# One-hot rows in groups, an earlier trial gather, early weights spread over more turns, and one copy on another engine

## The chip, the cores and the metric

The kernel runs on one core of one Trainium2 chip. The metric is device time in microseconds (us) of one execution. The engines are PE (TensorE), DVE (VectorE), ACT (ScalarE), POOL (GpSimd) and SP (SyncE, which here only issues DMAs); each takes its instructions in order, and they meet through semaphores. A queue letter behind an engine's name in the rows (ACTq, POOLq) is its sequencer, which waits, branches or issues.

## What is computed

Block-causal attention over 8 batches of 8 heads, 576 tokens and 64 columns a head, then a mixture of 8 experts over the 4608 tokens. Each expert takes at most `capacity` = 80 of the tokens that the gate sends to it, those with the largest gate weight; all other rows of the output are zero.

```python
scores = q @ k.T / 8, masked by blocks of 64          # per batch and head
attn   = softmax(scores) @ v
x      = attn.transpose(0, 2, 1, 3).reshape(4608, 512)
logits = x @ w_gate;  expert = argmax(logits);  g = softmax(logits)[expert]
for e in range(8):
    tok = the (at most) 80 tokens of expert e with the largest g
    out[tok] = g[tok] * (relu(x[tok] @ w1[e]) @ w2[e])
```

## The kernel before

**Attention.** The 64 heads are worked as 32 pairs, four pairs a batch. A loop runs over turns `i`; turn `i` holds steps of several pairs, written out in the list `TURN` as (distance, step): scores and softmax of pair i, transposes and values of pair i-1, preparation of q and k (`prep`) for pair i+2, loads of v for pair i+2 (`load_v`, three POOL DMAs), of k for pair i+5 (`load_k`, four POOL DMAs) and of q for pair i+6 (SP). The order on every engine is that of the program text (`tc.manual_schedule`). In every fourth turn and the one behind it POOL also stores the finished x of a batch to `xs` in HBM (`store_x`, L389, two and two DMAs). SP stores a batch's 1/sums (`rs`, L395 and L396), and clears the output from turn 4 on, 512 KB at a time, in three turns of four.

`prep` transposes q on DVE (L626) and scales it on POOL (L629, tile `T`); PE's scores (L648) read it. POOL's `pad` (L602, tile `VZ`) copies parts of v for the values (L784). The five transposes at L743 come once in a turn.

**Early weights.** Four of the sixteen weight matrices (2 MB each) are loaded by POOL during attention: `EARLY` says how many quarters are issued at the head of which turn (n = 32 is the number of pairs). At the head of a turn stands `early(EARLY.get(i, 0))`; a call with 1 to 3 issues single quarters of 512 KB at L346, one with 4 a whole matrix as one DMA. All later weights are issued by SP (L325).

**The last pair.** In turn n, ahead of the copy of the last pair's `xT` out of PSUM (`take` of "values", L792 on ACT or L794 on DVE, by the table `TAKE`), stand `recip` (DVE, L379 and L380) and `store(nc.scalar)`, which issues the two `rs` stores of the last batch from ACT's queue (L395, L396). Behind the copy come DVE's `flip` (L384), POOL's last four `xs` stores (L389), and the last logits (PE L406), which ACT copies to `lgT` (L412).

**Selection.** From the gate weights each of the 128 partitions keeps its 12 largest candidates. The rank of a candidate is counted among the others: by DVE for the first five (L977, `cnt`), by ACT for seven (L981). `pen` (POOL) puts away what is no candidate. Then a one-hot row `OH[:, i]` of 80 columns is made for each candidate, nine by DVE and three by POOL (L991), and twelve small matmuls (L996, into `pick`) turn them into token numbers `gi` (DVE, L1017). Behind each of the first four picks stands a filler matmul (`warm`, L804). Eight indirect gathers on POOL (`fetch`, L1007), one for each expert, bring the rows of `xs`. Just ahead of them stands a trial gather (L1012) of 16 rows, whose indices are zero; it reads `xs` too.

**Experts.** For each expert PE runs two products (L1124) over the gathered rows, and POOL scatters the result into the output (L1172).

Of the kernel before, what the change touches and what calls it, by code (L numbers as in the profile page):

```python
# [7 lines left out]
F32 = mybir.dt.float32  # L8
F32R = mybir.dt.float32r
BF16 = mybir.dt.bfloat16  # L10
I32 = mybir.dt.int32
U32 = mybir.dt.uint32
AF = mybir.ActivationFunctionType
ALU = mybir.AluOpType
# [4 lines left out]
P = 128  # L19
# [7 lines left out]
NCAND = 12  # L27
CHUNK = 80


TAKE = {"back": {"A": "a", "B": "a", "C": "a"}, "values": {0: "v"}}
# [122 lines left out]
def tile_attn_moe(ctx, tc, q, k, v, w_gate, w1, w2, capacity, out, xs=None, dbg=None):  # L154
    nc = tc.nc
    B, H, S, D = q.shape
    NTOK, DM = out.shape
    E, _, F = w1.shape
    NP = H // 2
# [17 lines left out]
    if xs is None:  # L177
        xs = dram.tile([NTOK, XW], F32, name="xs")

    sel = ctx.enter_context(tc.tile_pool(name="sel", bufs=1))  # L180
# [64 lines left out]
    iota_b = const.tile([P, 2, CHUNK], BF16, name="iota_b")  # L245
# [52 lines left out]
    def capacities():  # L298
        nc.vector.tensor_tensor(iota_c16, sameR, iota_c, op=ALU.mult)
        nc.vector.tensor_reduce(iota_r, iota_c16, axis=AX.X, op=ALU.add)  # L300
        nc.vector.scalar_tensor_tensor(cap, cf[:, 1:2], 4294967296.0, cf[:, 0:1], op0=ALU.mult, op1=ALU.add)
        nc.vector.tensor_tensor(caplt, iota_p, cap, op=ALU.is_lt)
# [8 lines left out]
    def weights(n, after=None, parts=PARTS, underway=UNDERWAY):  # L311

        nonlocal nw
        for _ in range(n):
            src, e = wlist[nw]
            w_ = wpools[nw % len(wpools)].tile([P, KP * F], F32, name="w")
            nw += 1
            wt_[src is w2, e] = w_ = w_.rearrange("p (a f) -> p a f", f=src.shape[2])
            if nw <= FW0:
                early_.append((w_, src[e].rearrange("(a p) f -> p a f", p=P)))  # L320
                continue
            view = src[e].rearrange("(a p) f -> p a f", p=P)
            na = w_.shape[1]
            for a in range(0, na, na // parts):
                load = nc.sync.dma_start(w_[:, a:a + na // parts], view[:, a:a + na // parts]).ins  # L325
                for before in ((after,) if after is not None else ()) + tuple(parts_[-underway:][:1] if len(parts_) >= underway else ()):
                    tc.add_manual_dep(load, before.name, mybir.DependencyInfo(
                        mybir.DependencyClass.Sync, mybir.DependencyReason.DATA))
                parts_.append(load)
# [6 lines left out]
    def early(n):  # L336

        nonlocal begun
        while n:
            if begun % PARTS == 0:  # L340
                weights(1)
            w_, view = early_[-1]
            na = w_.shape[1]
            m = min(n, PARTS - begun % PARTS) if n >= PARTS else 1
            a = slice(na * (begun % PARTS) // PARTS, na * (begun % PARTS + m) // PARTS)
            nc.gpsimd.dma_start(w_[:, a], view[:, a])  # L346
            begun += m
            n -= m
# [194 lines left out]
    batches = {}  # L543

    class Pair:
# [242 lines left out]

        def take(self, what, x):

            if TAKE[what][x] == "a" and not (self.i == n - 1 and x == "A"):
                nc.scalar.copy(*self.out.pop((what, x)))  # L792
            else:
                nc.vector.tensor_copy(*self.out.pop((what, x)))  # L794

    def warm(n, wt, after=None, w=identr, c=4):

        if not n:
            return
        with ExitStack() as order:  # L800
            if after is not None:
                order.enter_context(tc.issue_after(after.ins))
            for i in range(n):
                nc.tensor.matmul(wt[:, 0:c * P].rearrange("p (a c) -> p a c", c=P), lhsT=w,  # L804
                                 rhs=w.unsqueeze(1).broadcast_to([P, c, P]), start=(i == 0), stop=(i == n - 1))

    n = B * NP
    EARLY = {n - 8: 2, n - 7: 2, n - 6: 2, n - 5: 2, n - 4: 4, n - 3: 4}
    pairs = [Pair(i) for i in range(n)]

    nc.gpsimd.memset(wgd, 0.0)
# [2 lines left out]
    with tc.manual_schedule():  # L814
# [3 lines left out]
        for i in range(-6, n + 6):  # L818
# [12 lines left out]
            if i == 7:  # L831
                capacities()
            early(EARLY.get(i, 0))
            if i == n:
# [50 lines left out]
    vec = nc.vector  # L885
    pool = nc.gpsimd
# [7 lines left out]
    tw = dict(reuse_waits="tile")  # L894
    fwa = late.enter_context(tc.tile_pool(name="fwa", bufs=FWA, **right, **tw))
    wpools += [fwa] * FWA
    weights(2, underway=6)
    sel2 = late.enter_context(tc.tile_pool(name="sel2", bufs=1, **right, **tw))

# [3 lines left out]
    NH = NCAND // 2  # L903
# [3 lines left out]
    NV = 5  # L907
# [35 lines left out]
    pen = sel.tile([P, 2, NH], F32, name="pen")  # L943
    pool.tensor_scalar(pen, key, scalar1=0.0, scalar2=8192.0, op0=ALU.is_lt, op1=ALU.mult)
    pool.tensor_tensor(pen, pen, iota_c[:, 0:NH].unsqueeze(1).broadcast_to([P, 2, NH]), op=ALU.add)
    pen = pen.rearrange("p h i -> p (h i)")
# [22 lines left out]
    per_expert(RI[:, :, 0], hi_)  # L969
    per_expert(RI[:, :, 1], lo_)  # L970
    pool.tensor_copy(RI[:, :, 2], sb)
    none = sel.tile([P, 1], I32, name="none")
    pool.memset(none, 0)
    cnt = sel.tile([P, NCAND], F32, name="cnt")
    for i in range(NV):
        junk = sel2.tile([P, 2 * HC], BF16, name="junk", bufs=2)
        counted = vec.tensor_scalar(junk, pall[0][:, 0:2 * HC], scalar1=key[:, 0, i:i + 1], scalar2=None, op0=ALU.is_gt,  # L977
                                    op1=ALU.add, accum_out=cnt[:, i:i + 1])
# [4 lines left out]
    OH = sel2.tile([P, NCAND, CHUNK], BF16, name="OH")  # L983
    wt = ps_s4.tile([P, 2, 512], F32, name="ps4")
    warm(WARM[3], wt[:, 0], ranked)
    pick = ps_s.tile([P, 512], F32, name="ps")
    NQ = 3
    for n_, i in enumerate((*range(NV), *range(NH, NCAND), *range(NV, NH))):
        quiet = NH <= i < NH + NQ
        with ExitStack() if quiet else tc.issue_after(counted.ins):  # L990
            made = (pool if quiet else vec).tensor_scalar(  # L991
                OH[:, i], iota_b[:, int(i >= NV)], scalar1=pen[:, i:i + 1], scalar2=cnt[:, i:i + 1],
                op0=ALU.subtract, op1=ALU.is_equal)
        if quiet:
            last_made = made
        picked = nc.tensor.matmul(pick[0:CHUNK, 0:3 * E], lhsT=OH[:, i], rhs=RI[:, i].rearrange("p k e -> p (k e)"),  # L996
                                  start=(n_ == 0), stop=(n_ == NCAND - 1))
        if n_ < 4:
            warm(1, wt[:, n_ % 2], picked, c=2)
# [4 lines left out]
    xg = [fx.tile([CHUNK, XW], F32, name="xg", bufs=E) for _ in range(E)]  # L1004
# [3 lines left out]
            out=xg[e], out_offset=None, in_=xs[:, :], in_offset=bass.IndirectOffsetOnAxis(ap=index.bitcast(U32), axis=0),  # L1008
            bounds_check=NTOK - 1, oob_is_err=False).ins

    with tc.issue_after(last_made.ins):
        pool.indirect_dma_start(  # L1012
            out=xg[E - 1][0:16], out_offset=None, in_=xs[:, :],
            in_offset=bass.IndirectOffsetOnAxis(ap=none[0:16].bitcast(U32), axis=0),
            bounds_check=NTOK - 1, oob_is_err=False)
    with nc.allow_low_precision(reason="whole numbers"):
        vec.tensor_reduce(gi, pick[0:CHUNK, 0:2 * E].rearrange("s (k e) -> s e k", k=2), axis=AX.X, op=ALU.add)  # L1017
    fetches = [fetch(e, gi[:, e:e + 1]) for e in range(E)]
# [208 lines left out]
    with tc.If(again > 0):  # L1227
# [26 lines left out]
        cnt = gen.tile([P, 1], F32, name="cnt")  # L1254
# [33 lines left out]
        for i in range(2):  # L1288
# [4 lines left out]
                                   op0=ALU.mult, op1=ALU.add)  # L1293
# [30 lines left out]
        with tc.For_i(0, more, 1):  # L1324
# [25 lines left out]
            for e in range(E):  # L1350
                xe = gen.tile([CHUNK, XW], F32, name="xe")
                pool.indirect_dma_start(out=xe, out_offset=None, in_=xs[:, :],
                                        in_offset=bass.IndirectOffsetOnAxis(ap=gj.bitcast(U32)[:, e:e + 1], axis=0))
# [27 lines left out]
                for a in range(FP):  # L1381
# [4 lines left out]
                    out=out[:, :], out_offset=bass.IndirectOffsetOnAxis(ap=sj.bitcast(U32)[:, e:e + 1], axis=0),  # L1386
                    in_=ye, in_offset=None, bounds_check=NTOK - 1, oob_is_err=False)
# [30 lines left out]
```

## Time and profile before

| what | value |
|---|---|
| median of 3 runs | 410.42 us (409.87 to 411.64) |
| the profiled execution | 406.74 us, of which the span of the program's instructions is 404.9 us |
| busy | PE 378.3 us (93%), PEld 292.2, DVE 280.9, ACT 264.6, POOL 254.3 |
| mean granted TensorE clock | 0.986 of full speed |
| DMA | 84.46 MB, mean 209 GB/s; 94429 of 120124 packets under 512 B |

The profile is of one execution. A row of a timeline gives start, duration, engine, line, operation, output and inputs, shapes and count; brackets at its end hold the engine's idle time just before and what ended it. The chain is followed back from the last instruction, at each step to what released it.

### The profile page before, as it was taken

The page shows a single profiled execution, that of the slowest core. Times are in us where ns is not written, and L with a number is a line of the kernel's source. Part 1 is how long each engine was busy: PE and PEld are TensorE (multiplying, and loading weights), DVE is VectorE, ACT ScalarE, POOL GpSimd, SP SyncE. Part 2 cuts the span into 40 slices and gives each one's busy share as a digit, 9 for nine tenths or more (in the row PEclk, how much of TensorE's full clock was granted, in tenths as well). Part 3 has the DMA queues.
Part 4 walks back from the last instruction along what each step waited for, and adds up shares of the span by engine and source line. Part 5 has one row for each costly group of instructions (what it writes and reads, how often), then busy time and mean ns, then how long its engine had stood idle before and what let it go on. Part 6 is the DMA issues. An engine that isn't in the chain of part 4 may idle for free.

```text
span 404.9 us, 15556 instructions
## 1 busy us (share of the span) xinstructions
PE 378.3 (93%) x6351; PEld 292.2 (72%) x6351; DVE 280.9 (69%) x651; ACT 264.6 (65%) x700; POOL 254.3 (63%) x440
## 2 busy tenths in 40 slices
PE   8899999999999999999999996999897799999990
PEld 4576777767777777776777775777557798999980
DVE  5788989998998998999899896887663131111120
ACT  2799999999999999999899996798132011111000
POOL 7889987887997798798799778622677110000000
PEclk9999999999999999999999998999999999999996
DMA  9999999979979898897999999996737988989800
GB/s 142 149 150 152 153 179 206 206 151 203 223 152 213 208 177 179 173 212 167 198 213 237 241 232 322 294 319 212 214 118 226 289 271 279 330 294 309 307 20 22
DMA packets 120124, 84.46 MB, mean 209 GB/s; under 512 B 94429, under 2 KB 96477, under 8 KB 120048
## 3 DMA queue, kind: packets, MB, share of 16 engines
q1 hardware_dynamic: 102432, 45.55, 50.1%
q0 software_dynamic: 15808, 37.55, 38.3%
q8 instruction: 52, 0.85, 0.9%
q10 hardware_dynamic: 1808, 0.31, 0.4%
q14 instruction: 24, 0.20, 0.2%
HBM read 63.25 MB, written 20.33 MB: 206 GB/s over the span
## 4 chain that ended last, share of the span: by engine, by line
PE 76%; DMA 10%; POOL 6%; issue 3%; DVE 2%; ACT 0%; POOLq 0%; ACTq 0%; DVEq 0%
PE sc L648 21%; PE sc L784 19%; PE ps L1124 11%; PE sc L735 10%; PE av L1124 8%; DMA vn<-in_v_dram 4%; DMA xs<-rs 3%; DMA w<-in_moe_w_dram 2%; POOL ld L580 2%; PE sc L406 2%; PE sc L743 1%; PE pm L1167 1%; PE sc L425 1%; POOL vn L593 1%; PE pm L1137 1%
## 5 line engine op out<-in xcount | busy, mean ns | idle before, releaser
L705 ACT ACTIVATE P<-sc,negm 128x448 f32<-128x448 f32 (+3 forms) x256 | 146.0, 584 | 14.0 <-DVE negm L684 7.4
L684 DVE TENSOR_REDUCE negm<-sc 128x1 f32<-128x448 f32 (+4 forms) x224 | 127.1, 617 | 14.1 <-PE sc L655 12.5
L648 PE MATMUL sc<-T,T 64*128 64x64 f32 (+4 forms) x768 | 112.5, 417 | 5.7 <-POOL T L629 5.0
L648 PEld LDWEIGHTS sc<-T,T 64*128 64x128 f32 x768 | 71.3, 188 | 37.5 <-issue 24.8
L580 POOL DMA_DIRECT2D ld<-in_k_dram x120 | 81.7, 686 | 2.0 <-DMA w<-in_moe_w_dram 1.0
L792 ACT COPY PT<-sc 128x1024 f32<-128x1024 f32 x63 | 60.8, 1016 | 13.3 <-PE sc L735 12.5
L784 PE MATMUL sc<-PT,vn 128*64 128x128 f32 (+1 forms) x512 | 61.2, 381 | 0.6 <-ACT PT L792 0.6
L1172 POOL DMA_INDIRECT out_dram<-y,si x8 | 7.5, 933 | 73.7 <-DVE y L1168 60.3
L735 PE MATMUL sc<-ident,P 64*128 64x64 f32 x1280 | 53.6, 227 | 0.1
L705 ACT ACTIVATION_READ_ACCUMULATOR P<-sc,negm 128x1 f32 x256 | 53.0, 207 | 0.0
L784 PEld LDWEIGHTS sc<-PT,vn 128*64 128x64 f32 x512 | 34.0, 138 | 23.6 <-issue 22.4
L735 PEld LDWEIGHTS sc<-ident,P 64*128 64x128 f32 x1280 | 45.2, 138 | 3.0 <-ACT P L705 1.0
L626 DVE STREAM_TRANSPOSE T<-ld 128x576 f32<-128x576 f32 x62 | 47.3, 765 | 0.0
L629 POOL TENSOR_SCALAR T<-T 128x576 f32<-128x576 f32 x31 | 20.7, 668 | 32.9 <-DVE negm L684 16.9
L1124 PE MATMUL ps<-xsT,w 128*64 128x80 f32 x1024 | 40.1, 234 | 1.4 <-issue 1.4
L1159 DVE COPY yT<-av 128x320 f32<-128x320 f32 x7 | 3.4, 491 | 53.2 <-PE av L1124 53.2
L1124 PEld LDWEIGHTS ps<-xsT,w 128*64 128x64 f32 x1024 | 37.2, 137 | 3.6 <-issue 2.8
L593 POOL DMA_DIRECT2D vn<-in_v_dram x64 | 39.8, 628 | 0.0
L1124 PE MATMUL av<-hT,w 128*64 128x80 f32 x896 | 33.4, 233 | 2.4 <-issue 2.4
L1124 PEld LDWEIGHTS av<-hT,w 128*64 128x64 f32 x896 | 32.3, 137 | 2.9 <-issue 2.9
L1149 ACT ACTIVATE hT<-ps 128x320 f32<-128x320 f32 x16 | 7.0, 438 | 40.8 <-PE ps L1124 40.8
L794 DVE COPY xT<-sc 128x576 f32<-128x576 f32 x32 | 24.0, 750 | 11.4 <-PE sc L762 11.4
(191 smaller groups left out, 524.8 us busy)
## 6 DMA issues: line engine op xcount, KB each, us to landing
w<-in_moe_w_dram SPq DMA_DIRECT2D x48, 512.0 KB, 5.5
out_dram<-zero SPq DMA_DIRECT2D x18, 512.0 KB, 5.6
ld<-in_q_dram SPq DMA_DIRECT2D x124, 72.0 KB, 4.7
ld<-in_k_dram POOLq DMA_DIRECT2D x120, 72.0 KB, 4.8
xs<-Y POOLq DMA_DIRECT2D x28, 288.0 KB, 5.5
vn<-in_v_dram POOLq DMA_DIRECT2D x32, 128.0 KB, 5.2
vn<-in_v_dram POOLq DMA_DIRECT2D x64, 64.0 KB, 4.7
w<-in_moe_w_dram POOLq DMA_DIRECT2D x8, 512.0 KB, 7.3
```

Of the source, the lines that this page charges most:

```text
L580: eng.dma_start(self.nat[x][r], (q, k)[x][self.b, self.h0 + h, :, 32 * i:32 * i + 32] .rearrange("(g r) d -> r g d", r=32))
L593: nc.gpsimd.dma_start(self.vn[c * BLK:(c + 1) * BLK, 1], turned[:, :, 1 - c])
L626: nc.vector.transpose(t, self.nat[x].rearrange("p g d -> p (g d)"))
L629: nc.gpsimd.tensor_scalar(t, t, scalar1=SCALE, scalar2=1.0, op0=ALU.mult, op1=ALU.mult)
L648: nc.tensor.matmul(to[h], lhsT=self.T[0][r, q:q + P], rhs=self.T[1][r, k0:k1], start=start, stop=stop)
L684: nc.vector.tensor_reduce(to, src, axis=AX.X, op=ALU.max, negate=True)
L705: nc.scalar.activation(dst, src, AF.Exp, bias=self.negm[0:n, u, h:h + 1], scale=1.0, accum_out=self.bt.sums[0:n, u, self.h0 + h:self.h0 + ...
L735: nc.tensor.transpose(pt[:, c, to(c, n_)], row[u][r, h, k(u, h, j):k(u, h, j) + P], ident[r, r])
L784: nc.tensor.matmul(to, lhsT=lhs, rhs=rhs, start=(n_ == 0), stop=(n_ == len(steps) - 1))
L792: nc.scalar.copy(*self.out.pop((what, x)))
L794: nc.vector.tensor_copy(*self.out.pop((what, x)))
L1124: yield nc.tensor.matmul(dst(b)[64 * c:64 * (c + 1)], lhsT=w_[:, a, col:col + 64], rhs=x_[:, a], start=(a == 0 and b == 0), stop=(a == n - ...
```

## The change

Four edits:

- `EARLY` gives one quarter to each of the turns n-16 to n-7 whose number is not 3 modulo 4 (16, 17, 18, 20, 21, 22, 24, 25), where it gave two to each of n-8 to n-5. The whole matrices in turns n-4 and n-3 stay.
- `take` lets ACT copy the last pair's `xT`, where DVE did.
- The trial gather is issued behind POOL's last `xs` store, into a tile of its own, and reads 16 rows of `q` instead of `xs`.
- The one-hot rows: a sum `cnt + pen` in bf16 for a group of candidates, then one `tensor_tensor` (is_equal) for several candidates at once, on DVE: 5 candidates, then 4 and 1. POOL makes two rows (it made three) as before.

```diff
-            if TAKE[what][x] == "a" and not (self.i == n - 1 and x == "A"):
+            if (TAKE[what][x] == "a") != (self.i == n - 1 and (what == "values" or x == "A")):
                 nc.scalar.copy(*self.out.pop((what, x)))
             else:
                 nc.vector.tensor_copy(*self.out.pop((what, x)))
...
-    EARLY = {n - 8: 2, n - 7: 2, n - 6: 2, n - 5: 2, n - 4: 4, n - 3: 4}
+    EARLY = {**{i: 1 for i in range(n - 16, n - 6) if i % NP < NP - 1}, n - 4: 4, n - 3: 4}
...
+    none = sel.tile([16, 1], I32, name="none")
+    pool.memset(none, 0)
+    trial = sel.tile([16, D], F32, name="trial")
+    with tc.issue_after(batches[B - 1].stored.ins):
+        pool.indirect_dma_start(
+            out=trial, out_offset=None, in_=q.rearrange("b h s d -> (b h s) d"),
+            in_offset=bass.IndirectOffsetOnAxis(ap=none.bitcast(U32), axis=0),
+            bounds_check=NTOK - 1, oob_is_err=False)
     weights(2, underway=6)
...
-    NQ = 3
+    NQ = 2
+    groups = (((0, NV), ((0, NV),)), ((NV, NCAND), ((NH + NQ, NCAND), (NV, NH))))
+    for (a, b), cuts in groups:
+        with tc.issue_after(counted.ins), nc.allow_low_precision(reason="whole numbers, exact up to 256"):
+            vec.tensor_tensor(sum_[:, a:b], cnt[:, a:b], pen[:, a:b], op=ALU.add)
+            for c0, c1 in cuts:
+                vec.tensor_tensor(OH[:, c0:c1], iota_b[:, int(c0 >= NV)].unsqueeze(1).broadcast_to([P, c1 - c0, CHUNK]),
+                                  sum_[:, c0:c1].unsqueeze(2).broadcast_to([P, c1 - c0, CHUNK]), op=ALU.is_equal)
+    for i in range(NH, NH + NQ):
+        pool.tensor_scalar(OH[:, i], iota_b[:, 1], scalar1=pen[:, i:i + 1], scalar2=cnt[:, i:i + 1],
+                           op0=ALU.subtract, op1=ALU.is_equal)
     for n_, i in enumerate((*range(NV), *range(NH, NCAND), *range(NV, NH))):
-        quiet = NH <= i < NH + NQ
-        with ExitStack() if quiet else tc.issue_after(counted.ins):
-            made = (pool if quiet else vec).tensor_scalar(
-                OH[:, i], iota_b[:, int(i >= NV)], scalar1=pen[:, i:i + 1], scalar2=cnt[:, i:i + 1],
-                op0=ALU.subtract, op1=ALU.is_equal)
-        if quiet:
-            last_made = made
         picked = nc.tensor.matmul(pick[0:CHUNK, 0:3 * E], lhsT=OH[:, i], rhs=RI[:, i].rearrange("p k e -> p (k e)"),
...
-    with tc.issue_after(last_made.ins):
-        pool.indirect_dma_start(
-            out=xg[E - 1][0:16], out_offset=None, in_=xs[:, :],
-            in_offset=bass.IndirectOffsetOnAxis(ap=none[0:16].bitcast(U32), axis=0),
-            bounds_check=NTOK - 1, oob_is_err=False)
```

## Rows read from the trace of the kernel before

**Rows 1.** Chain that ended last, in order of time: start us, us, what.

```profile
234.62 8.89 DMA vn<-in_v_dram
...
287.50 12.36 DMA xs<-rs
```

**Rows 2.** Timeline of PE: once-a-turn transposes, and one wait.

```profile
212.29 0.41 PE L743 MATMUL sc<-ident,P 64*128 64x64 f32 x5
...
220.63 0.29 PE L743 MATMUL sc<-ident,P 64*128 64x64 f32 x3
...
245.90 0.41 PE L743 MATMUL sc<-ident,P 64*128 64x64 f32 x5
249.40 1.02 PE L648 MATMUL sc<-T,T 64*128 64x448 f32 x4 [3.09 <-POOL T L629]
...
258.78 0.47 PE L743 MATMUL sc<-ident,P 64*128 64x64 f32 x5
```

**Rows 3.** Timeline of POOL in turn 24.

```profile
214.72 1.14 POOL L346 DMA_DIRECT2D w<-in_moe_w_dram  x2
...
216.66 0.78 POOL L590 DMA_DIRECT2D vn<-in_v_dram  x1
217.43 1.26 POOL L593 DMA_DIRECT2D vn<-in_v_dram  x2
...
219.39 2.07 POOL L580 DMA_DIRECT2D ld<-in_k_dram  x3
221.85 0.67 POOL L580 DMA_DIRECT2D ld<-in_k_dram  x1 [0.39 <-DMA w<-in_moe_w_dram]
```

**Rows 4.** Timelines of DVE, POOL, ACT and PE in the selection.

```profile
294.68 0.20 POOL L934 COPY cand<-cand 128x12 f32<-128x12 f32 x1 [3.29 <-DVE cand L911]
294.89 0.61 DVE L923 TENSOR_TENSOR spread<-near,sameR 128x192 f32<-128x192 f32 x2
295.29 0.34 POOL L944 TENSOR_SCALAR pen<-key 128x12 f32<-128x12 f32 x1
...
298.64 2.03 DVE L991 TENSOR_SCALAR OH<-iota_b,pen,cnt 128x80 bf16<-128x80 bf16 x9
298.88 1.36 POOL L991 TENSOR_SCALAR OH<-iota_b,pen,cnt 128x80 bf16<-128x80 bf16 x2
299.06 0.36 PE L804 MATMUL ps<-identr 128*128 128x256 f32 x1
299.29 0.36 PE L804 MATMUL ps<-identr 128*128 128x256 f32 x1
299.36 0.23 ACT L981 ACTIVATION_READ_ACCUMULATOR junk<-av,keyn 128x1 f32 x1
...
300.77 1.05 POOL L1012 DMA_INDIRECT xg<-xs,none  x1 [0.54 <-issue]
300.97 0.17 DVE L1017 TENSOR_REDUCE gi<-ps 80x8 int32<-80x16 f32 x1 [0.30 <-PE ps L996]
302.13 1.00 POOL L1007 DMA_INDIRECT xg<-xs,gi  x1 [0.30 <-issue]
```

**Rows 5.** Stretches of four turns: us, busy by engine, PEclk, DMA share, GB/s.

```profile
118.60:152.20 33.60, 33.58 (x515) 24.89 (x515) 31.10 (x67) 31.15 (x83) 27.94 (x47) 1.00 0.90 191
203.60:237.20 33.60, 33.58 (x517) 24.89 (x515) 31.09 (x68) 31.15 (x83) 28.98 (x49) 1.00 1.11 226
```

**Rows 6.** Timelines of DVE, ACT and PE around the last copy of xT.

```profile
286.94 0.69 DVE L794 COPY xT<-sc 128x576 f32<-128x576 f32 x1
287.50 0.66 ACTq L396 DMA_DIRECT2D xs<-rs  x1
287.69 1.16 PE L406 MATMUL sc<-xT,wgd 128*32 128x384 f32 x10 [0.82 <-DVE xT L794]
```

**Rows 7.** Groups by line and form: busy us, mean ns of one, idle before.

```profile
L412 ACT COPY lgT<-sc 128x576 f32<-128x576 f32 x7 | 4.5, 643 | 0.0
```

**Rows 8.** Timeline of ACT at the start of the program.

```profile
2.68 1.28 ACT L618 ACT_TABLE_LOAD   x1 [2.68 <-issue]
```

More of the change, by code (lines that the diff above doesn't have):

```diff
@@ L971, in tile_attn_moe @@
     pool.tensor_copy(RI[:, :, 2], sb)
-    none = sel.tile([P, 1], I32, name="none")
-    pool.memset(none, 0)
     cnt = sel.tile([P, NCAND], F32, name="cnt")
+    sum_ = sel2.tile([P, NCAND], BF16, name="sum")
     for i in range(NV):
```

## The prediction

> **What bounds the kernel now.** I read three views in this order. The page's 40 slices show TensorE busy in nearly every slice, with two weak places in the attention part: one slice near 246 us and the slices from 283 to 306 us, where selection runs. The chain that ended last says what those two places wait for: ahead of the first stands a DMA of v that took 8.89 us, in the second the last store of 1/sums, 12.36 us from issue to landing [rows 1]. The timeline then gives sizes.
>
> First place. Each turn of the pair loop has one group of five transposes at L743, a good clock for the loop. From 212.29 to 220.63 one turn takes 8.34 us; the turn at the same place of the four-turn cycle a cycle and more later runs from 245.90 to 258.78, 12.88 us, and inside it TensorE sits 3.09 us waiting for POOL's T [rows 2]. So 12.88 - 8.34 = 4.54 us are lost there; what exceeds the 3.09 us is the work behind it. POOL is late because its queue is in order and it waits for its own transfers. In turn 24 it issues w, w, three pieces of v and three of k, eight transfers, and the ninth stands 0.39 us until the first w has landed [rows 3]. I read that as eight transfers in flight for this queue; the later waits have the same form. Two pieces of 512 KB a turn make these landings late, and from turn to turn the lateness adds up until the slack of T is gone.
>
> Second place. The trial gather reads xs, so it stands behind the landing of the rs store; it starts at 300.77 and ends at 301.82, and only then the first real gather goes, at 302.13. Its index gi was ready at 300.97 + 0.17 = 301.14 [rows 4]. Behind the gather comes the expert part, where the chain is TensorE nearly throughout, so what is won or lost before the gather reaches the end one to one.
>
> **The change, part by part.**
>
> Early pieces. Eight single pieces move from turns 24 to 27, two each, to turns 16, 17, 18, 20, 21, 22, 24 and 25, one each; the two whole matrices of turns 28 and 29 stay. The same eight POOL issues are made, only earlier. Removed: the stall, -4.54 us. Added: traffic in turns that had none. Four normal turns (33.6 us) have a summed DMA busy share of 0.90; the four turns up to 237 us, with six pieces in them, 1.11, and TensorE is busy for 33.58 of 33.60 us in both [rows 5]. So a piece costs about 0.21 x 33.6 / 6 = 1.2 us of all sixteen engines; three in four turns make 0.90 + 3 x 1.2 / 33.6 = 1.01, well under the 1.11 that TensorE did not feel. With one piece a turn, the transfer eight back is that piece itself one turn (8.4 us) earlier; the first piece of turn 24 landed within 221.85 - 214.72 = 7.1 us [rows 3], so POOL should hardly wait. I take 0 us for the added traffic, covered by the loads' lead of two to four turns; if that cover is gone, a stall like the removed one, up to 4.54 us, comes back. Value -4.5, bounds -4.6 and 0. Next late in turn 28 is TensorE itself.
>
> Last x copied by ACT. Today VectorE copies xT of the last pair from 286.94 to 287.63, and the last logits wait for it [rows 6]. On ACT the copy of the same shape takes 0.64 us [rows 7], no shorter. But in program order the two rs stores come first on ACT, and they wait for the reciprocal; the second is issued from 287.50 to 288.16 [rows 6]. At the kernel's start ACT has three loads of k to issue, and its first instruction, a table load that waits for no data, begins only at 2.68, held by issue all that time [rows 8]: an issue holds the queue. So the copy runs from about 288.2 to 288.85, 1.2 us later than now, and the logits, the gate, the picks and the gather behind it are a string of dependent steps without slack: +1.2 us. Bounds: +1.3, and 0 if the issue held only its first moments. Also queued behind the copy on ACT is lgT, which needs it anyway; VectorE's flip and POOL's last four xs stores wait for it as well, but they stand behind the same traffic that holds the rs store until 287.50 + 12.36 = 299.86 [rows 1], so I expect their landing to move little.
>
> Trial gather. It leaves the place just ahead of the real one. The first real gather then starts when gi is there, plus about the 0.3 us that stand ahead of such a transfer [rows 4]: 301.44 instead of 302.13, -0.7 us. It now waits itself for the rs landing, over a microsecond ahead of gi, so nothing. In its new place it takes 1.05 us of POOL, in a gap where POOL stands idle for 3.29 us before L934 [rows 4]; without that cover POOL's constants for the picks would be up to 1.35 us late.
>
> One-hot rows. Removed: nine VectorE instructions, 2.03 us together, and one of POOL's three [rows 4]. Added: two small sums and three tensor_tensor over 400, 320 and 80 elements. The nearest row is two tensor_tensor of 192 elements, broadcast operands too, in 0.61 us [rows 4]; by elements that is 0.64, 0.51 and some 0.2 us. First group: counts done near 298.7, where the rows start now, sum to 298.9, rows to 299.55. Second: ACT's last count ends at 299.59 [rows 4], sum to 299.8, rows to 300.5 or so. The rows are ready 0.2 us sooner than 300.67. But the first pick now starts at 299.55 instead of 299.00, and four filler matmuls, 0.23 us apart [rows 4], stand between the first five picks: fifth pick near 300.5, last ended near 301.0, gi near 301.2. That is +0.1 us; bounds -0.3 (fillers overlapped) and +0.7 (next paragraph).
>
> A row and a rule speak against the groups. POOL's pen (L944, 12 elements a partition) ran from 295.29 beside a tensor_tensor of VectorE that ended at 295.50, and took 0.34 us, where its like L934 took 0.20 [rows 4]: held by some 0.14 us, perhaps. If a group and one of POOL's two remaining OH rows (0.68 us each [rows 4]) held each other whole, VectorE could lose up to 0.7 us there, and gi as much: rival (b). The Trainium skill, SBUF — State Buffer, section "SBUF: two separate sides", states just that: VectorE with two SBUF inputs and a GpSimd operation that reads SBUF lock each other out of a shared pair of ports for a whole instruction. The row agrees in kind; it can't show the length.
>
> **Sum.** -4.5 (stall) + 1.2 (x on ACT) - 0.7 (trial) + 0.1 (groups) = -3.9 us. The profiled execution took 406.74 us (span 404.94 and 1.8 around it) and would take 402.8. The runs' median, 410.42, is 3.7 us above it, and I can't see where those lie; I subtract the same 3.9 us: 406.5.
>
> **Rivals.**
> (a) ACT's issue does not hold the copy. It speaks for it that only two issues are in the way, against it the start of the kernel. Then +0.1 instead of +1.2: -5.0, 405.4 us.
> (b) VectorE's groups and POOL's OH rows hold each other: +0.7 instead of +0.1, so -3.3, 407.1 us. For it: the 0.14 us of L944; against it: VectorE may come first, and then POOL alone waits, with time to spare.
> (c) The stall is not the pieces' doing, or the turn stalls as long at another place: nothing won, +0.6 remains, 411.0 us. For it: turn 27 also holds two xs stores and the gate's sp on POOL; against it: the same turn of earlier cycles, with those, takes 8.34 us.
> (d) Slower: POOL's ring fills in the xs turns. Turns 18 and 22 put w, three v, four k and two xs, ten transfers, through the eight places, beside a clear of 512 KB. If a piece then lands later than a turn (8.4 us) after its issue, each later issue waits, and T comes late in turns 19 and 23 and once more at 26: three stalls of up to 3 us, and one gone: 3 x 3 - 4.5 + 0.6 = +5, 415.5 us. It decides from a landing of 8.4 us on; v took 8.89 at two pieces a turn [rows 1], 7.1 is what the first piece alone took.
> (e) The clock: TensorE's longer pause before the last logits (0.82 us now [rows 6], 2.0 then) is followed by a lower granted clock, as the page's slice of the 3.09 us pause shows one; some of the logits at half speed, +1 us, 407.5. It is within the range.
>
> **Chances.** Forecast 0.50, (a) 0.11, (b) 0.12, (e) 0.05, (c) 0.13, (d) 0.09. The forecast's own range is 405 to 408; (a), (b) and (e) lie in it or beside it. The range for 8 in 10 leaves out (c) and (d) only and adds what the median's unexplained 3.7 us may hold (if the timed runs stall longer, more is won): 403.6 to 409.6. A difference under 0.5%, 2.05 us, is about what a measurement of this kernel can't tell from none. Faster by more: 0.50 + 0.11 + 0.12 + 0.05 = 0.78; the same, (c), 0.13, to which a part of (d) that just balances adds 0.01; slower 0.08.
>
> **What would show it.** Right: the L743 groups are about 8.3 to 8.9 us apart through turn 28, POOL has no wait on a transfer before 245 us, the granted clock stays full near 246 us. ACT's copy of xT starts when its L396 ends. The trial starts before L934, and the real gather 0.3 us behind gi; VectorE has three OH instructions, and the fillers fix the fifth pick. Wrong: POOL waiting on w or v in turns 18 to 26, TensorE idle on T or VZ there, an xs or rs landing later than gi, or a pause on TensorE at first picks that lowers its clock.

## The result, and the profile after

| what | before | after |
|---|---|---|
| median of four runs each | 411.03 us (409.87 to 417.26) | 404.29 us (403.54 to 405.07) |
| the profiled execution | 406.74 us, span 404.9 | 404.40 us, span 402.6 |
| mean granted TensorE clock | 0.986 | 0.982 |

The ratio is 0.9845 with a 95% interval of 0.981 to 0.9881, which is 6.4 us less (4.9 to 7.8). It is of mean times and, like those below, leaves out executions over 1.5% above the fastest of their kernel, such as before's 417.26 us. Forecast were -3.9 us and 406.5, range 403.6 to 409.6: the direction and the range held, and the gain is 2.5 us larger than the sum. The two profiled executions differ by 2.3 us only, so what the profiles show is less than the sum, and what the timings show is more. Both differences are taken apart below.

**The stall of turn 28 is gone.** Timeline of TensorE after, the once-a-turn transposes that answer to [rows 2]:

```profile
238.86 0.42 PE L743 MATMUL sc<-ident,P 64*128 64x64 f32 x5
246.69 0.41 PE L743 MATMUL sc<-ident,P 64*128 64x64 f32 x5
255.02 0.29 PE L743 MATMUL sc<-ident,P 64*128 64x64 f32 x3
```

The turn that took 12.88 us takes 255.02 - 246.69 = 8.33, and there is no wait on `T`. The stretches that now hold the pieces, as in [rows 5] (start and end, length, busy time of PE, PEld, DVE, ACT and POOL, granted clock, DMA share, GB/s):

```profile
153.00:186.60 33.60, 33.58 (x515) 24.87 (x515) 31.08 (x67) 31.12 (x83) 28.83 (x49) 1.00 1.08 229
186.60:220.20 33.60, 33.59 (x516) 24.90 (x515) 31.10 (x67) 31.12 (x83) 29.93 (x51) 1.00 1.10 231
204.40:238.00 33.60, 33.59 (x517) 24.89 (x515) 31.15 (x68) 31.13 (x83) 29.13 (x49) 1.00 1.14 228
```

The DMA share is 1.08 to 1.14, not 1.01, and TensorE is busy as before. POOL still waits for its own transfers. Between 130 and 262 us it does so seven times, 4.4 us in all, from 175 us on; before it was seven times and 6.15 us, all from 221 us on. The prediction had named such waits in turns 18 to 26 as a sign of being wrong. From POOL's timeline (answers to [rows 3]):

```profile
199.89 0.62 POOL L593 DMA_DIRECT2D vn<-in_v_dram  x1 [0.90 <-DMA vn<-in_v_dram]
...
215.91 0.60 POOL L346 DMA_DIRECT2D w<-in_moe_w_dram  x1
...
224.00 0.57 POOL L346 DMA_DIRECT2D w<-in_moe_w_dram  x1 [1.28 <-DMA w<-in_moe_w_dram]
...
231.91 0.79 POOL L590 DMA_DIRECT2D vn<-in_v_dram  x1 [0.23 <-DMA w<-in_moe_w_dram]
```

The piece issued at 215.91 held the queue until about 223.7, some 7.8 us. That is close to the turn of 8.4 us from which rival (d) would have begun, and it cost 1.28 us that POOL had to spare. In e2 below, the piece of turn 18 took 8.8 us to land, and no turn behind it is longer for that: the threshold of (d) was passed without its price.

**The last xT is later, and the clock falls.** Timelines of ACT and PE around it (answers to [rows 6]), and the stretch behind it:

```profile
283.24 0.42 ACTq L395 DMA_DIRECT2D xs<-rs  x1
283.70 0.73 ACTq L396 DMA_DIRECT2D xs<-rs  x1
284.48 0.64 ACT L792 COPY xT<-sc 128x576 f32<-128x576 f32 x1 [4.67 <-issue]
285.17 1.52 PE L406 MATMUL sc<-xT,wgd 128*32 128x384 f32 x10 [2.11 <-ACT xT L792]
...
285.80:289.20 3.40, 3.40 (x12) 2.43 (x11) 1.66 (x7) 0.80 (x2) 2.67 (x5) 0.50 1.04 363
```

ACT's copy starts where the second store's issue ends. TensorE pauses for 2.11 us where it paused for 0.82, and 0.6 us later the granted clock is 0.50 for 3.4 us, its 1.2 GHz level. The longer pause alone does not do this: it is 2.08 us in e3, 2.22 in e7 and 2.01 in e10, and behind these the clock stays at 1.00; behind 2.10 in e6 it falls.

**The selection.** Timelines of POOL, DVE and PE (answers to [rows 4]):

```profile
289.16 0.98 POOL L901 DMA_INDIRECT trial<-in_q_dram,none  x1 [0.30 <-issue]
292.53 0.20 POOL L942 COPY cand<-cand 128x12 f32<-128x12 f32 x1 [2.39 <-DVE cand L919]
...
296.72 0.65 POOL L1003 TENSOR_SCALAR OH<-iota_b,pen,cnt 128x80 bf16<-128x80 bf16 x1
296.89 0.67 DVE L1000 TENSOR_TENSOR OH<-iota_b,sum 128x400 bf16<-128x400 bf16 x1
297.62 0.21 PE L1006 MATMUL ps<-RI,OH 128*80 128x24 bf16 x1 [0.81 <-DVE OH L1000]
297.75 0.64 DVE L1000 TENSOR_TENSOR OH<-iota_b,sum 128x320 bf16<-128x320 bf16 x2
299.05 0.17 DVE L1022 TENSOR_REDUCE gi<-ps 80x8 int32<-80x16 f32 x1 [0.65 <-PE ps L1006]
299.50 1.08 POOL L1017 DMA_INDIRECT xg<-xs,gi  x1 [2.13 <-DVE gi L1022]
```

The trial lies in POOL's gap, the rows come in three instructions, and the first real gather starts 0.28 us behind `gi` (0.99 before).

**Balance of the two profiles, at the first real gather.** It starts at 299.50 where it started at 302.13, 2.63 us sooner: -4.55 for the stall; +0.8 for two turns near the start of the loop that paused longer, before any piece is loaded; +1.29 for xT; +0.36 for the logits at the lower clock; +0.23 from the first count to `gi`; -0.71 for the gather behind `gi`; the remaining -0.05 is rounding. From the gather to the end the kernel takes 103.1 us (102.8 before). Two larger differences nearly cancel in this: to the end of the last scatter it takes 97.8 us where it took 94.4 (the last section tells of that), and from there to the end 5.3 where it took 8.4.

**The end of the program.** The last scatter, and the instructions named DRAIN at the end of the program on POOL's queue (durations in ns: shortest, median, longest; then the first and last start in us), before and then after:

```profile
395.59 0.92 POOL L1172 DMA_INDIRECT out_dram<-y,si  x1 [3.35 <-DVE y L1168]
L1413 POOLq DRAIN  x3: 46/103/3831, 400.3 to 404.7; - x3
...
396.38 0.91 POOL L1177 DMA_INDIRECT out_dram<-y,si  x1 [3.35 <-DVE y L1173]
L1418 POOLq DRAIN  x3: 46/103/1212, 400.5 to 402.3; - x3
```

The longest drain takes 1.21 us where it took 3.83, and that is 2.6 of the 3.1 us by which the end is shorter. It is the same to the ns in other profiles: 3831 in e1 and e3, 1212 in each run with the new `EARLY`, but 1457 in e8 and 722 in e9. So it goes with how the pieces are issued. What it waits for is not shown. The prediction has no such term.

### The profile page after: what moved, and what is told of

Read it like the earlier page. It is cut to its first block, busy times and chain, and to the rows that moved or that the text cites. A ratio compares the mean times of both kernels' runs of the same rounds, so it can differ in the third digit from the quotient of the medians.

```text
span 402.6 us, 15555 instructions
## 1 busy us (share of the span) xinstructions
PE 380.8 (95%) x6351; PEld 295.1 (73%) x6351; DVE 279.7 (69%) x646; ACT 264.9 (66%) x701; POOL 252.7 (63%) x439
## 4 chain that ended last, share of the span: by engine, by line
PE 85%; POOL 5%; issue 3%; DVE 2%; DMA 2%; ACT 0%; ACTq 0%; POOLq 0%; DVEq 0%
PE sc L648 23%; PE sc L784 21%; PE ps L1129 11%; PE sc L735 10%; PE av L1129 8%; PE sc L406 2%; POOL ld L580 2%; DMA vn<-in_v_dram 2%; PE sc L743 2%; PE sc L425 2%; PE sc L804 1%; PE pm L1172 1%; POOL vn L593 1%; PE pm L1142 1%; PE sc L762 1%
## 5 line engine op out<-in xcount | busy, mean ns | idle before, releaser
L1129 PE MATMUL ps<-xsT,w 128*64 128x80 f32 x1024 | 43.0, 241 | 4.6 <-issue 4.6
L1129 PEld LDWEIGHTS ps<-xsT,w 128*64 128x64 f32 x1024 | 39.9, 143 | 7.1 <-issue 6.4
```

What stands on the lines that cost most here:

```text
L1129: yield nc.tensor.matmul(dst(b)[64 * c:64 * (c + 1)], lhsT=w_[:, a, col:col + 64], rhs=x_[:, a], start=(a == 0 and b == 0), stop=(a == n - ...
```

## The experiments

They ran on three chips, each group beside runs of the kernel before: e1 to e4 on one (before: 404.73 us median), e5 to e8 on a second (409.85), e9 to e12 on a third (409.24). Theory: the eight pieces hold up POOL's in-order queue, ACT's issues hold the copy of xT, and the other two edits are small. Rivals: the traffic itself is what stalls, and the gain comes from the other edits.

| run | ratio to before (95%) | us saved | turn 28, us | last values to first gather, us | last scatter to end, us |
|---|---|---|---|---|---|
| e1 before again | 1.0016 (0.9968 to 1.0065) | -0.6 | 10.19 | 15.83 | 8.38 |
| e2 early pieces alone | 0.9873 (0.9822 to 0.9923) | 5.1 | 8.34 | 15.87 | 5.50 |
| e3 the other three edits | 0.9993 (0.9955 to 1.0031) | 0.3 | 11.90 | 16.97 | 8.52 |
| e4 after, xT on VectorE | 0.9858 (0.9806 to 0.9911) | 5.7 | 8.34 | 15.72 | 5.13 |
| e5 after, xT first on ACT | 0.9834 (0.9793 to 0.9875) | 6.8 | 8.3 | 15.52 | 5.24 |
| e6 after, trial in the old place | 0.9837 (0.9794 to 0.9879) | 6.7 | 8.3 | 17.52 | 5.36 |
| e7 after, single rows | 0.9846 (0.9806 to 0.9886) | 6.3 | 8.3 | 17.01 | 5.08 |
| e8 before, pieces of 1 MB | 0.9924 (0.9892 to 0.9955) | 3.1 | 9.65 | 16.02 | 5.52 |
| e9 before, pieces issued by SP | 0.9864 (0.982 to 0.9908) | 5.6 | 8.34 | 16.00 | 4.13 |
| e10 after again | 0.9908 (0.9879 to 0.9938) | 3.8 | 8.35 | 16.90 | 5.04 |
| e11 xT first, stores on SP | 0.9846 (0.9805 to 0.9887) | 6.3 | 8.3 | 14.61 | 5.30 |
| e12 as e11, fillers ahead | 0.9837 (0.9795 to 0.9878) | 6.7 | 8.3 | 14.39 | 5.23 |

"us saved" is one minus the ratio, times the median of before on that chip. "Turn 28" is the distance of its L743 groups, "last values" the end of the last L762, "last scatter" the end of POOL's last instruction for the output. These three are of the profiled execution and from unrounded times, so up to 0.01 off the rows shown; in before they were 12.88, 16.19 and 8.43, in after 8.33, 17.37 and 5.29.

**e1.** The kernel before, unchanged.

> The kernel before, unchanged, profiled once more. Theory: the stall at the turn of pair 28 is part of every execution; the L743 groups of pairs 27 and 28 stand 12 to 13 us apart again, with TensorE waiting about 3 us for T. The earlier profile took 406.74 us while the timed runs had a median of 410.4 to 411.0. Theory: the 4 us between lie in the expert part, which then takes some 107 us from the first gather to the end instead of 102.8. Rival: they lie in a longer stall at pairs 27 and 28 (16 to 17 us between the groups).

The stall is there again, and smaller, as TensorE's timeline shows:

```profile
246.62 0.41 PE L743 MATMUL sc<-ident,P 64*128 64x64 f32 x5
249.05 1.19 PE L648 MATMUL sc<-T,T 64*128 64x448 f32 x8 [2.02 <-POOL T L629]
256.81 0.47 PE L743 MATMUL sc<-ident,P 64*128 64x64 f32 x5
```

256.81 - 246.62 = 10.19: 1.85 us over an undisturbed turn, where the profile of before lost 4.5. The stall is no constant; a single execution doesn't size it. The expert part took 102.5 us and not 107, so neither theory of the gap between profile and median is borne out; on this chip there is no such gap (profile 404.12 us, median 405.48).

**e2 and e3**, the change cut in two.

```diff
 # e2: before, with
-    EARLY = {n - 8: 2, n - 7: 2, n - 6: 2, n - 5: 2, n - 4: 4, n - 3: 4}
+    EARLY = {**{i: 1 for i in range(n - 16, n - 6) if i % NP < NP - 1}, n - 4: 4, n - 3: 4}
 # e3: after, with the first of these two lines
```

> The kernel before with the new EARLY alone. Theory: the whole gain comes from here; 4.5 us less than before (a ratio near 0.989), the groups of pairs 27 and 28 stand 8.3 us apart. Rival 1: the spread of pieces wins more than the stall shows (6 us or more, ratio 0.985 or less), because in most runs of before the stall is longer. Rival 2: without the other edits nothing is won, since the next wait (the rs landing ahead of the trial gather) takes the time back; ratio 1.00.

> The changed kernel with the old EARLY. Theory: the stall of about 4.5 us is back and the other three edits together are worth nothing (x on ACT +1.3 and its clock +0.4, trial -0.7, rows +0.2): within 1.5 us of before. Rival: the other three edits hold the 2.4 us that were won beyond the forecast; then this is 2 us or more below before.

The pieces alone save 5.1 us (3.1 to 7.2); the three other edits together are worth nothing that can be measured (-1.3 to 1.8 saved; the sum gave 0.6 lost). Where the pieces' gain lies, the profiles of e1 and e2 tell: the span falls from 402.3 to 397.1 us, by 5.2. Of that 1.85 are the stall, 0.8 the start-up pause and 2.9 the end of the program, and the experts give back 0.3. In e3 the stall is back at its place, and the long drain too:

```profile
248.53 1.19 PE L648 MATMUL sc<-T,T 64*128 64x448 f32 x8 [2.09 <-POOL T L629]
```

So rival (c) falls, and the gain is the pieces', but only a part of it is the stall.

**e9 and e8**, what it is about the pieces. Both are the kernel before with two pieces a turn in turns 24 to 27. In e9 SP issues them; in e8 POOL issues each two as one transfer of 1 MB.

```diff
 # e9
-            nc.gpsimd.dma_start(w_[:, a], view[:, a])
+            (nc.gpsimd if m == PARTS else nc.sync).dma_start(w_[:, a], view[:, a])
 # e8
-            m = min(n, PARTS - begun % PARTS) if n >= PARTS else 1
+            m = min(n, PARTS - begun % PARTS)
```

> The kernel before, with the same quarters in the same turns 24 to 27, but issued from SP's queue. The traffic is the same; POOL's queue holds eight transfers fewer. Theory: the stall at pairs 27 and 28 comes from POOL waiting, in order, for places behind the large transfers; without them on its queue POOL waits hardly at all, the groups of pairs 27 and 28 stand 8.3 to 8.9 us apart, and the time is 2 to 5 us below before, as with the new EARLY alone. Rival: the traffic makes k, v and q late whoever issues it; then the groups stand 10 us or more apart and the time is that of before.

> The kernel before with the same bytes in the same turns, but each turn's two quarters as one transfer of 1 MB: four fewer transfers on POOL's queue in turns 24 to 27. Theory: what stalls is POOL's queue, which allows eight transfers in flight; with one transfer less a turn POOL waits less and the 4.5 us stall shrinks to under 2 us. Rival: the traffic itself is late (v, k behind 1 MB in the DMA engines' queues); then the stall stays at 4 us or more.

Rows of e9, of the stretch that [rows 5] ends with and of its timeline:

```profile
203.60:237.20 33.60, 33.58 (x515) 24.89 (x513) 31.10 (x67) 31.13 (x83) 27.87 (x47) 1.00 1.10 229
...
211.60 2.61 SPq L346 DMA_DIRECT2D w<-in_moe_w_dram  x2
...
246.13 0.41 PE L743 MATMUL sc<-ident,P 64*128 64x64 f32 x5
254.48 0.28 PE L743 MATMUL sc<-ident,P 64*128 64x64 f32 x3
```

The same pieces in the same turns move at the same DMA share (1.10, before 1.11), and turn 28 takes 254.48 - 246.13 = 8.35 us. From turn 24 on POOL waits for no piece in that profile. So the traffic is not what stalls; the queue in which the pieces stand is. Two things are taken from POOL at once, the waits (6.15 us in before) and the issuing of eight pieces (4.5 us), and no run parts them. The 5.6 us saved can't size the stall either, since the end of the program is 4.3 us shorter than in before. e8 settles less. With half as many issues the stall is 1.3 us, less than in e1 by 0.5, where e1 and before differ by 2.7, and one wait on a piece is longer than any in before:

```profile
242.52 1.32 POOL L389 DMA_DIRECT2D xs<-Y  x2 [3.79 <-DMA w<-in_moe_w_dram]
...
248.39 1.19 PE L648 MATMUL sc<-T,T 64*128 64x448 f32 x8 [1.48 <-POOL T L629]
```

POOL's waits on transfers in turns 24 to 27 add up to 6.2 us in e8 and 6.15 in before: fewer issues, each longer to land (9.1 us for the one whose landing the trace holds, where single pieces took 7.3 on the median). Of the 3.1 us that e8 saves, the end of the program can be 2.9. That the ninth transfer waits for the first of eight agrees with the waits shown here (after's `w` at 215.91, three of v, four of k, then the wait at 224.00), but e8 didn't test it cleanly. The semaphore numbers in the trace tell where the eight come from: POOL's transfers use eight semaphores in turn (111 to 118), and each waits for the landing of the one that used its semaphore last. So the limit is one that the program sets; that a queue of the chip has eight places is not shown.

**e4 and e5**, the copy of xT.

```diff
 # e4: after, with
-            if (TAKE[what][x] == "a") != (self.i == n - 1 and (what == "values" or x == "A")):
+            if TAKE[what][x] == "a" and not (self.i == n - 1 and x == "A"):
 # e5: after, with
                 if taken and j == n - 1:
                     batches[B - 1].recip()
-                    batches[B - 1].store(nc.scalar)
                 getattr(pairs[j], what)(*args)
+                if taken and j == n - 1:
+                    batches[B - 1].store(nc.scalar)
```

> The changed kernel with the last xT copied by VectorE again. Theory: ACT's copy waits behind its two rs stores, so VectorE's is done 1.3 us sooner, and the pause of TensorE before the last logits falls from 2.1 to 0.8 us and its clock stays full there: 1.3 to 1.7 us less than the changed kernel, about 402.7 us. Rival: the time is the same, because the landing of the rs or xs stores takes over ahead of the gather.

> The changed kernel, with ACT copying the last xT before it issues the two rs stores (recip stays where it is on VectorE). Theory: the copy is held by the stores' issue alone; it then starts within 0.1 us of the end of the last value matmul (L762), 2.3 us sooner than in the changed kernel, and the stores leave at about the same time as now. The gather comes 2.3 us sooner unless the rs landing, about 12.4 us behind its issue, then ends last: 1.5 to 2.5 us less than the changed kernel. Rival: ACT's copy itself is late for another reason (its source, its place behind PF); then it starts at 2.5 us behind L762 as now and nothing is won.

With xT on VectorE the copy starts 0.99 us behind the last L762 (2.34 in after), the clock holds, and the gather comes 15.72 us behind it instead of 17.37. With the copy ahead of the issues on ACT (e5's timeline):

```profile
281.86 0.64 ACT L792 COPY xT<-sc 128x576 f32<-128x576 f32 x1 [2.37 <-PE sc L762]
282.93 0.42 ACTq L395 DMA_DIRECT2D xs<-rs  x1
283.39 0.80 ACTq L396 DMA_DIRECT2D xs<-rs  x1
284.23 0.70 ACT L412 COPY lgT<-sc 128x384 f32<-128x384 f32 x2 [1.74 <-PE sc L406]
```

xT is done 2.3 us sooner, but now `lgT` starts only when the second issue has ended (284.19): the issue holds whatever copy stands behind it. Both runs say the same: rival (a) falls, and ACT's copy is not dear, ACT's issues ahead of it are.

**e6 and e7**, the two small edits undone one by one.

```diff
 # e6: after, with the trial ahead of the first fetch again
-    with tc.issue_after(batches[B - 1].stored.ins):
-        pool.indirect_dma_start(out=trial, ..., in_=q.rearrange("b h s d -> (b h s) d"), ...)
...
+    with tc.issue_after(last_made.ins):
+        pool.indirect_dma_start(out=xg[E - 1][0:16], ..., in_=xs[:, :], ...)
 # e7: after, with the twelve single rows of before (nine on VectorE, three on POOL)
```

> The changed kernel with the trial gather back ahead of the real one, reading xs. Theory: the first real gather starts behind the trial, some 1.0 us behind gi instead of 0.28: 0.7 us more than the changed kernel. Rival: the trial's old place cost more than its own time, since it also bound the picks' POOL rows to the landing of rs; then 1.5 us or more.

> The changed kernel with the old one-hot rows, nine on VectorE one by one and three on POOL. Theory: from the first count to gi 4.2 us as in the kernel before, against 4.4 in the changed one, since the fillers between the picks now run behind the late first pick: 0.2 us less than the changed kernel, too little for the time to show. Rival: the groups win time that their order hides; 0.3 us or more above the changed kernel.

e6's timeline, POOL's last row, trial and first gather:

```profile
295.92 0.66 POOL L997 TENSOR_SCALAR OH<-iota_b,pen,cnt 128x80 bf16<-128x80 bf16 x1
296.76 1.05 POOL L1016 DMA_INDIRECT xg<-xs,none  x1 [0.18 <-issue]
298.26 0.17 DVE L1021 TENSOR_REDUCE gi<-ps 80x8 int32<-80x16 f32 x1 [0.63 <-PE ps L1000]
298.71 1.00 POOL L1011 DMA_INDIRECT xg<-xs,gi  x1 [0.91 <-DVE gi L1021]
```

The trial ends at 297.81, before `gi` at 298.43, and the gather follows by 0.28 us as in after. So moving the trial is worth nothing here. It starts 0.18 us behind POOL's last row, and POOL makes two rows and not three: that row ends 2.58 us behind the first count, where it ended 3.29 behind it in before, and `gi` is later by 0.24. Where POOL makes three rows and the trial is in its old place, it also starts right behind the last of them (0.23 to 0.54 us), and the gather follows `gi` by 0.66 to 0.99 us (before, e1, e2, e8, e9), so there the move would be worth 0.4 to 0.7. In e7 the single rows take 4.31 us from first count to `gi`; the groups in after take 4.41. No gain or loss of either edit shows in the times.

**e10, e11 and e12**, after again beside two versions that take the issues off ACT and the fillers out of the picks.

```diff
 # e11: e5, with the two stores issued by SP
-                    batches[B - 1].store(nc.scalar)
+                    batches[B - 1].store(nc.sync)
 # e12: e11, with the four fillers ahead of the picks
-    warm(WARM[3], wt[:, 0], ranked)
+    warm(WARM[3] + 2, wt[:, 0], ranked)
...
-        if n_ < 4:
-            warm(1, wt[:, n_ % 2], picked, c=2)
```

> The changed kernel once more, on the chip and beside the runs on which the next two are timed. Theory: 4 to 7 us below before, the spread being that of the stall of before. If the slow first expert product (single matmuls 0.7 to 1.4 us apart some 6 to 11 us behind the first gather, and a lower granted clock behind them) belongs to the chip, it is in all four profiles of this job or in none; if it belongs to the changed kernel, it is in this one and the next two, and not in the one with the early quarters on SP.

> The changed kernel, with ACT copying the last xT first and SP issuing the two rs stores. Theory: ACT's queue holds neither xT nor lgT back; xT is there 2.3 us sooner than in the changed kernel, lgT follows without a wait, and rs lands within some 4 us as the seven earlier ones from SP do, being ahead of the weights in SP's ring. The gather comes 2.5 to 3.5 us sooner against the end of the last value matmul (17.4 us in the changed kernel, 15.5 with x first and the stores still on ACT): 2 to 3 us less than the changed kernel. Rival: SP's two weight matrices, now queued behind the stores, start 1.7 us later and the experts wait for them; then nothing is won at the end.

> As the one with the rs stores on SP, and the four short filler matmuls between the first picks are taken out and put, as two long ones, ahead of the picks. Theory: with the rows made in groups the fillers set the fifth pick; without them the last pick is set by VectorE's last row, and first count to gi takes 4.0 to 4.1 us instead of 4.4. Rival: the last row, not the fillers, ends last already; then 4.4 us stay. In both cases the whole changes by 0.4 us at most, under what the times can show.

On this chip the unchanged after saves 3.8 us (2.5 to 5.0), a little under what was expected. With the stores on SP nothing holds ACT, and `lgT` starts 1.60 us behind the last L762 (e11's timeline, with the one-hot rows of the same run):

```profile
283.46 0.70 ACT L412 COPY lgT<-sc 128x384 f32<-128x384 f32 x2 [0.92 <-PE sc L406]
...
293.96 0.57 DVE L1002 TENSOR_TENSOR OH<-iota_b,sum 128x400 bf16<-128x400 bf16 x1
...
294.13 0.91 POOL L1005 TENSOR_SCALAR OH<-iota_b,pen,cnt 128x80 bf16<-128x80 bf16 x1
```

The gather comes 2.3 us sooner than in e10. e11's expert part was 1.6 us longer than e10's in the profiled executions, so the profile shows only part of it; the medians say 402.35 against 404.89. In e12 first count to `gi` is 4.10 us, against 4.31 in e11 and 4.41 in after: the fillers between the picks were worth 0.2 us once the rows come in groups, and 0.1 had gone with e11 already. e12's median is 401.46 us, 3.4 less than after on the same chip, and its interval (0.9795 to 0.9878) ends where e10's (0.9879 to 0.9938) begins: it beats both kernels.

## Why the prediction was right, and where it was off

**Early pieces (-4.5): right in place and cause, in size by luck.** The stall is gone, and e9 shows that POOL's queue and not the traffic was the cause. But e2's 5.1 us are not the forecast 4.5: in the profiles of that chip the stall is 1.85 us, and 2.9 us lie at the end of the program, which the prediction put at nothing by not having it. The stall was taken from one execution as if fixed; in the four profiles with the pieces in turns 24 to 27 on POOL (before, e1, e3, e8) it was 4.5, 1.85, 3.6 and 1.3 us, and the longest is the one that was read. Two terms inside were mis-sized too. The DMA share was put at 1.01 and is 1.08 to 1.14: I took one stretch of 0.90 as the ground of all, but before's stretch from 152.20 to 185.80 us has 0.94, and three pieces add 0.14 to it, 1.6 us a piece instead of 1.2. And "POOL should hardly wait" took the first landing, 7.1 us, for all; the one I could follow took 7.8 us, and POOL waited up to 1.28 us at a time and 4.4 us in all. T's slack took it, so the 0 us for added traffic held, by less margin than the text said. The "eight transfers in flight" are eight semaphores of the program.

**Last x on ACT (+1.2): right.** Behind the last L762 the copy comes 1.3 us later, at the end of the second issue, as the table load of [rows 8] let one expect. Rival (e), which I gave 0.05, came true beside it, at +0.36 us and not +1: the clock was low for 3.4 us, but from 287.6 on TensorE only ran fillers in it (L804). The longer pause was in my own sum, so it deserved more weight, though not that of a term: the clock fell in two of the five profiles with that pause (after and e6; not e3, e7, e10), and only in after beside the logits.

**Trial (-0.7): right against its own `gi`, worth nothing in this kernel.** 0.28 us instead of 0.99 was forecast as 0.3. But the step read the trial as standing behind the landing of rs. That landing came at 299.86 [rows 1], and POOL's last row ended at 298.88 + 1.36 = 300.24 [rows 4]; the trial stood behind the row, and the landing can have added some 0.4 us at most (0.54 us from row to trial, where e1, e2, e6, e8 and e9 have 0.18 to 0.44). The step also treated the edits as independent. The groups edit takes one of three rows from POOL, which brings the trial 0.7 us sooner, and makes `gi` 0.2 us later; e6 shows that with these two the trial costs nothing in its old place.

**Groups (+0.1): measured +0.2.** The rows took 0.67 and, two together, 0.64 us, where the estimate had 0.64 and 0.71, and the fillers set the picks, as e12 confirms. Rival (b) happened at a seventh of its price. In after the group of 400 elements starts beside POOL's second row and takes 0.67 us; in e11 and e12, where it starts ahead of that row and lies beside the first for 0.2 us only, it takes 0.57 and that row 0.91 in e11 instead of 0.65. So the one that comes second loses 0.10 (DVE) or some 0.25 us (POOL). By the Trainium skill, SBUF — State Buffer, section "SBUF: two separate sides", the second "fully blocks" until the first is done; then after's group would have waited from 296.89 to 297.37, 0.48 us. The traces agree that they disturb each other, not that one waits out the other.

**The sum.** In the profiles the span fell by 2.3 us instead of 3.9. The 1.6 us between are the start-up pause (0.8), the clock (0.36), the groups (0.13) and the expert part (0.27), in which 3.4 us lost in the experts and 3.1 won at the end of the program stand against each other. In the timings 6.4 us were saved in the comparison above and 3.8 in e10. The second fits the sum in size, but not in its terms: if before ends on that chip as in its other profiles (8.4 us behind the last scatter), the end of the program is 3.4 us of it, and the stall a good deal less than 4.5. For the first I kept the same 3.9 us for the median, though before's median lay 3.7 us above its profile, after's 0.1 us below its own. What lies in those 3.7 us is not shown. The matmuls described below would fill them if before's timed runs had them, as after's profile and e8 do and before's profile does not; no trace of those runs is kept. The text named a longer stall as a reason to widen the range downward; the result lies in that part, but a longer stall is not shown.

## What to carry to other kernels

A transfer that POOL issued in order was paid for by everything behind it once its eight semaphores were taken: spread big loads over turns, or put them on a queue that nothing urgent shares, and look for waits of the issuing engine on its own transfers. Where two copies seem equal on two engines, look at what stands ahead of each in program order, DMA issues too (0.4 and 0.7 us each here). Edits on one dependent string don't add up: the wait on the trial counted only as long as POOL made a third row ahead of it. And follow a gain to the last instruction: a drain at the end of the program was 2.6 us shorter here, for a change 150 us and more ahead of it; in the loop alone it can't be seen, and the stall would get the credit.

## What the runs showed of the hardware

The first expert's matmuls can crawl. In after's chain of work (start, length, what) 40 of them run at speed and then go one at a time:

```profile
303.92 1.59 PE ps L1129 x40
305.51 1.18 issue
306.69 0.23 PE ps L1129
306.92 1.22 issue
308.13 0.23 PE ps L1129
308.36 0.51 issue
308.88 0.23 PE ps L1129
...
309.70:316.50 6.80, 5.62 (x73) 5.17 (x74) 0.76 (x2) 0.86 (x2) 2.29 (x9) 0.50 1.05 285
```

TensorE waits for nothing that the trace shows, 0.5 to 1.2 us before each, and then has the lower clock for 6.8 us (last row). The same pattern stands in e5 to e12, on the second and third chip, in variants of before as in those of after; e8's chain has it:

```profile
305.37 1.09 issue
306.47 0.23 PE ps L1124
306.70 1.18 issue
```

It is in none of e1 to e4 and not in the profile of before. From the first gather to the end of the last scatter the nine profiles with it take 96.8 to 99.9 us, the five without 93.6 to 94.5, so some 4 us; from the first gather to the end, the drain included, 103.2 and 101.2 on the mean. So it goes with where or when a kernel ran and not with the change; its cause was not found.
